# Neighborhood attention on Trainium2: the first load of a band moved behind a turn by DMA, and a V item ahead of a P V

## The chip, the cores and the metric

The kernel runs on one core of a Trainium2 chip. A core has five engines with their own instruction queues: TensorE (PE: matmuls and, overlapping them, weight loads), VectorE (DVE), ScalarE (ACT), GpSimd (POOL) and SyncE (SP). Here SP computes nothing: it issues DMAs, in the order of its queue. Engines wait for each other by semaphores. Matmuls write to PSUM, and VectorE and ScalarE empty it to SBUF. The metric is the device time of one execution in microseconds (us); lower is better.

## The reference: what is computed

An image of 224 x 224 pixels with 192 channels (bf16) gets dilated neighborhood attention: each pixel attends to 7 x 7 = 49 pixels around it, two apart in each direction; at the border the window is pushed inside.

```python
qkv = x @ wqkv
r0 = jnp.clip(ir - half, 0, H - 1 - (ks - 1) * dil)      # half = 6, ks = 7, dil = 2
...
kn = ... # the 49 keys of each pixel, by rows r0 + 2a and columns c0 + 2b
vn = ... # and their values
logits = jnp.einsum('bnc,bnkc->bnk', qf, kn) * scale
p = _softmax(logits, axis=-1)
o = jnp.einsum('bnk,bnkc->bnc', p, vn) @ wo
```

There is one head. The inputs are x (1 x 224 x 224 x 192), wqkv (192 x 576) and wo (192 x 192), all bf16.

## The kernel before, in words

**Tiles.** Since the dilation is two, the image falls into classes of even and odd rows and columns. The work goes over 14 *steps* (seven row tiles times two row classes), each of seven *pairs* m = 0 to 6, 98 pairs k in all. A pair has two strips (`ab` = 0, 1), and each strip has two column classes. The products Wq Wk^T and Wv Wo are formed once at the start, so that a step needs `G` (queries times Wq Wk^T), the image itself as keys (`XA`, `XB`), and `VV` (values times the output weights).

**One pair.** `stage1` (line 499) makes the scores s of a strip on TensorE, with mask rows in the same matmuls, and takes the row maxima nmx on VectorE (line 501). `stage1b` (line 508) makes the exponentials p on ScalarE. `stage2` turns p round, so that it can be a weight of the next matmul. In most pairs that is done by 16 transposes on TensorE (line 538) and a copy from PSUM (line 539); in the pairs that the table `TURN` lists, a DMA transpose issued by SP does it (line 522). In steps 2 to 10 these are pairs 4 and 5 (`turned`), in steps 11 and 12 pairs 2 to 6, in step 13 pairs 0 and 1. `stage3` (line 548) is P V: 16 matmuls for a pair into one of two PSUM buffers for each strip. `stage4` divides by the row sums on VectorE (lines 554 and 571) into one of six output buffers `o_sb`, which SP stores (line 577); the border strip's stores go from GpSimd (line 600).

**Lag.** From k = 14 on the P V of pair k - 3 is done in the turn of the loop for pair k (`values_of`). So P V of pair 5 of a step falls into pair 1 of the next step, and that of pair 4 into pair 0.

**Background work.** While a step's pairs run, the values (`v_item`, lines 335, 338, and the copy out of PSUM at 326 or 328) and the G items (lines 415 and 450) of the next step are made between them. The table `BACK` says which go with which pair: its first entry, if it is not "-", is issued in the middle of the pair (`w64`), the others at its end (`w128`). For pair 1 of a step the entry is "v10e v11 v12e v13e": v10 is the first, in the middle, behind P V. PSUM buffers for these items are three, used in turn. Three moves of values from one row tile's buffer to the other's (`v_over`, line 349) follow the V items 6, 9 and 13; the first two are DMAs from SP in pairs 6 and 0, the third a copy on GpSimd.

**Loads.** A *band* is 16 image rows. `load_items(b)` (lines 145 to 156) gives three DMA transposes from SP (line 154), 448 KB each: for bands from 4 on first the middle 128 channels into `X1[b]`, one of two staging buffers, then the first and the last 128 into `XA`, which is a ring of six bands. At pair 0 of step n the three loads of band n + 3 are made ready, and one is issued at the very end of each of the pairs 0, 1 and 2. From `X1` GpSimd copies the middle channels to `XB` (line 160, at pair 2 of step n for band n + 3) and sorts all three parts into `XS` (line 170) for the V items: for band n + 3 at pairs 2 and 4, and at pair 3 those of band n + 2, in the other class. That copy at pair 3 is the last reader of `X1[n + 2]`.

**Order.** `in_order` keeps every engine's instructions in the order of the program. In SP's queue stand the loads, the turns, the moves of values and the stores of `o_sb`, one behind the other. Each is issued when those ahead of it are issued and its own semaphores are there.

Of the kernel before, what the change touches and what calls it, by code (L numbers as in the profile page):

```python
# [23 lines left out]
NBAND = 14  # L24
# [75 lines left out]
def kernel(  # L100
# [44 lines left out]
    def load_items(b):  # L145

        src = xp[16 * b:16 * b + 16].rearrange("r j c -> (r j) c")
        at = (16 * b) % (2 * RP) * S

        def one(k):  # L150
            if k == 1:
                X1[b] = x1_p.tile([128, BND], BF, name=f"x1_{b}", tag="x1")
            dst = X1[b][:] if k == 1 else XA[k // 2][:, at:at + BND]
            nc.sync.dma_start_transpose(out=dst.unsqueeze(1), in_=src[:, 128 * k:128 * k + 128])  # L154

        return [lambda k=k: one(k) for k in ((0, 2, 1) if b in (0, 2, 3) else (1, 0, 2))]
# [183 lines left out]
    def v_item(rc, ti, cb):  # L340
        def emit(dve):
            pv = ps_g.tile([128, 512], F32, name="pv", tag="pg")
            v_mms(pv, lambda k, h: XS[rc][:, k, cb, 64 * h:64 * h + 64])
            evac(_win(VV[rc][ti % 2], 0, 128, AT[cb] * VP, [[193, 2], [1, C]]), pv[:, 0:2 * C].rearrange("p (t c) -> p t c", c=C), dve)
        return emit

    def v_over(rc, ti, c0, c1, eng=nc.sync.dma_start):

        eng(out=VV[rc][1 - ti % 2][0:64, c0:c1, :], in_=VV[rc][ti % 2][0:64, c0:c1, :])
# [126 lines left out]
    def stage1(J, ab):  # L476
        s = 2 * J.m + ab
        s_ps = SS[ab]


        cols = {0: [(1, 7, S - 7), (8, 8, 0)], 2: [(1, 15, 9)]}.get(s, [(2, 14, 8 * s - 6)])
        lo = cols[0][0]
        for cc in range(2):
            units = []
            for h in range(2):
                u = []
                for pas in range(2):
                    X = (XA, XB)[pas][cc]
                    for (v, k0, n) in key_rows(J, h):
                        for (q, nq, c) in cols:  # L490
                            o = _win(s_ps, 64 * h, 64, cc * 256 + 16 * k0 + q, [[16, n], [1, nq]])
                            u.append((n * nq, o, G[J.rc][cc][:, pas, s, 64 * h:64 * h + 64], _win(X, 0, 128, _x(J.rc, v, c), [[RW, n], [1, nq]]), pas))
                units.append(u)
            done = [0, 0]
            while units[0] or units[1]:
                h = 0 if units[0] and (done[0] <= done[1] or not units[1]) else 1
                (cols_, o, w, r, pas) = units[h].pop(0)
                done[h] += cols_
                nc.tensor.matmul(o, lhsT=w, rhs=r, start=(cc == 0 and done[h] == cols_), stop=(cc == 1 and not units[h]), skip_group_check=True)  # L499
        nmx = stat.tile([128, 2], F32, name="nmx", tag="nmx")  # L500
        nc.vector.tensor_reduce(out=nmx[:], in_=_win(s_ps, 0, 128, lo, [[256, 2], [16, 16], [1, 16 - lo]]), axis=AX.XY, op=ALU.max, negate=True)  # L501
        J.p = PP[J.k % 3]
        J.s[ab] = (s_ps, nmx)
# [9 lines left out]
    def turned(J):  # L513
        return J.m in TURN[J.n]
# [37 lines left out]
    def stage4a(J, ab):  # L552
        J.rs[ab] = stat.tile([128, 2], F32, name="rs", tag="rs")
        nc.vector.reciprocal(out=J.rs[ab][:], in_=J.o_ps[ab][:, C:C + 2])
        return J.rs[ab]
# [55 lines left out]
    def g_all(n):  # L611
        ti, rc = steps[n]
        its = [g_items(rc, ti, s0, ns) for (s0, ns) in GROUPS]
        return [it for (w0, w1, h) in its for it in (w0, w1)], [h for (w0, w1, h) in its]
# [85 lines left out]
    ld, gw, vs = [], [], []  # L700

    def back(it, by_dve):
        it(by_dve)
        for (i, c0, c1) in ((7, 0, 8), (10, 8, 11), (13, 11, 14)) if nb == 0 or nb >= 11 else ((6, 0, 6), (9, 6, 10), (13, 10, 14)):
            if it in vs and it is vs[i]:
                v_over(rcb, tib, c0, c1, pool if nb >= 11 or nb > 0 and i in (13,) else nc.sync.dma_start)

    def values_of(k):

        if k <= 12 or k > 96:  # L710
            return [k - 2] if k >= 2 else []
        return [] if k == 13 else [k - 3, k - 2] if k == 96 else [k - 3]

    for k in range(NP + 2):
        J = pairs[k] if k < NP else None
        n = J.n if J else NSTEP
        w64, w128 = [], []
        if J:
            m = J.m
            nb, mb = divmod(k - LAG, 7)  # L720
            bg = k >= LAG and nb + 1 < NSTEP
            if bg and mb == 0:
                tib, rcb = steps[nb + 1]
                gw, gh = g_all(nb + 1)
                vs = [v_item(rcb, tib, cb) for cb in (0, 1, 2, 3, 4, 5, 6, 13, 7, 8, 9, 10, 11, 12)]
            if n == 0:
                w64 = gh0[m + 1:m + 2] if m < 3 else gh[mb // 2:mb // 2 + 1] if mb % 2 == 0 else []
                w64 = [(it, False) for it in w64]
            elif bg:
                w = [(({"g": gw, "h": gh, "v": vs}[t[0]][int(t[1:].rstrip("de"))], t[-1] == "d" or t[-1] == "e" and turned(pairs[k - 1])) if t != "-" else None) for t in (SECOND if nb == 0 else BACK if nb < 11 else LATE)[mb].split()]  # L730
                w64, w128 = [it for it in w[:1] if it], w[1:]
            stage1(J, 0)
            stage1(J, 1)
            stage1b(J, 0)
            if m == 0 and n + 3 < NBAND:
                ld = load_items(n + 3)
        if k == NP:
            stage2(pairs[k - 1])
        late = [pairs[i] for i in values_of(k)]
        for A in late[:1]:  # L740
            stage3(A, 0)
            stage3(A, 1)
            if k >= NP:
                stage4a(A, 0)
                stage4a(A, 1)
            stage4(A, 0)
            if k == NP - 1:
                stage4a(A, 1)
        for (it, by_dve) in w64:
            back(it, by_dve)  # L750
        if J:
            stage1b(J, 1)
        if J and turned(J):
            stage2(J)
        if 1 <= k < NP and not turned(pairs[k - 1]):
            stage2(pairs[k - 1])

        if late and n > 0:
            stage4(late[0], 1)
        for A in late[1:]:  # L760
            stage3(A, 0)
            stage3(A, 1)
            stage4(A, 0)
            stage4(A, 1)
        if not J:
            continue

        for w in PLAN[m].split() if n == 0 else ():
            (kind, by), at = w.split(":")[0], [int(c) for c in w.split(":")[1:]]
            if kind in "VWGH":  # L770
                {"V": v0, "W": vs, "G": gw0, "H": gw}[kind][at[0]](by == "d")
            elif kind == "N" and late:
                stage4(late[0], 1)
            elif kind == "X":
                xb_items(2, act if by == "a" else dve)[at[0]]()
            elif kind == "R":
                v_over(0, 0, at[0], at[1], nc.scalar.dma_start if by == "a" else nc.sync.dma_start)
            elif kind == "T":
                v_over(rcb, tib, at[0], at[1], nc.scalar.dma_start if by == "a" else nc.sync.dma_start)
        for (it, by_dve) in w128:  # L780
            back(it, by_dve)
        if ld:
            ld.pop(0)()
        if n == 0 and m == 1:
            first_vd()
            g_row_on(1, 2, 12)
            g_col_on()
        for q in range(2):
            if (n, m) == ((1, 3), (1, 5))[q]:
                marks_on(q)  # L790
        add = [it for c in FIRST[k] for it in first_pool(c)] if k < len(FIRST) else []
        if n > 1:
            if m == 3 and n + 2 < NBAND:
                add = sort_items(n + 2, J.rc, pool)
            if m in (2, 4) and n + 3 < NBAND:
                srt = sort_items(n + 3, J.rc, pool)
                add = srt[:2] if m == 4 else xb_items(n + 3, pool) + srt[2:]
        pool_q[:0] = add
        if n == 12 and m == 1:
            last = ((0, 9, 0, 1), (9, 7, 9, 0))  # L800
            g_col(1, 6, 0, 1, pool)
            g_row(1, 6, 0, 1, pool, last)
            g_row(1, 6, 1, 13, pool, last[1:])
        pool_do(max(4 if n < NSTEP - 1 else 8, len(add)))
# [34 lines left out]
```

## Time and profile before

| | |
|---|---|
| median of 3 runs | 338.47 us (338.19 to 339.24) |
| the profiled execution's own time | 340.54 us |
| its span, first to last instruction | 338.8 us |
| granted TensorE clock, mean | 0.994 |
| busy: TensorE, VectorE, ScalarE, GpSimd | 318.8, 310.4, 306.3, 286.4 us |
| SP's DMA queue, share of 16 DMA engines | 82.9% |

Times in a view are microseconds from the start of the span. A row of a timeline has the start, the duration, engine and line, the operation, the tile written <- the tiles read, the shapes, and how many instructions were merged into the row; in brackets the idle time before it and who ended it. "SPq" is SP's queue: its duration runs from when the queue comes to the instruction to when the DMA is issued, not to its landing. A row of waits has total, times and longest. A row of the chain of waits has start, duration and what the end of the program waited for at that time; a "DMA" row there runs from the issue to the landing.

### The profile page before, as it was taken

What the parts mean: (1) busy time and instruction counts of PE and PEld (TensorE: products, weight loads), DVE (VectorE), ACT (ScalarE), POOL (GpSimd) and SP (SyncE); (2) the same over time, 40 slices, a digit from 0 to 9 for tenths busy, and PEclk for the clock granted to TensorE, in tenths of its full rate; (3) what the DMA queues carried; (4) which work ended last, traced back from release to release, by engine and by line L of the source; (5) the groups of instructions that cost most, each with busy time, mean ns of one, the idle gap of its engine ahead of it and who ended that gap; (6) DMA issues with size and microseconds to landing.
All of it is one profiled execution on the core that took longest, in us unless ns stands there. A gap on an engine that the chain in (4) does not pass through costs nothing.

```text
span 338.8 us, 18840 instructions
## 1 busy us (share of the span) xinstructions
PE 318.8 (94%) x7820; PEld 291.3 (86%) x7820; DVE 310.4 (92%) x730; ACT 306.3 (90%) x807; POOL 286.4 (85%) x428
## 2 busy tenths in 40 slices
PE   4499999999999999999999999999999999999982
PEld 2378898999999999998999999988899889999871
DVE  8759999989999999998999999999999989999992
ACT  7679899999999999898999999999999989999982
POOL 8399999899989969889698897994996978997664
PEclk9999999999999999999999999999999999999997
DMA  8999745999979998899997998979879978959634
GB/s 173 207 194 185 140 99 127 196 226 183 168 186 188 176 192 155 158 206 146 166 183 165 179 180 186 160 160 190 160 162 177 159 177 131 143 111 161 130 100 100
DMA packets 143368, 55.78 MB, mean 165 GB/s; under 512 B 117113, under 2 KB 141138, under 8 KB 143283
## 3 DMA queue, kind: packets, MB, share of 16 engines
q1 hardware_dynamic: 138207, 51.98, 82.9%
q0 software_dynamic: 4416, 1.81, 2.9%
q8 instruction: 61, 1.00, 1.3%
q10 hardware_dynamic: 660, 0.80, 1.0%
q14 instruction: 24, 0.20, 0.2%
HBM read 0.29 MB, written 19.27 MB: 58 GB/s over the span
## 4 chain that ended last, share of the span: by engine, by line
PE 73%; ACT 8%; DMA 4%; DVE 4%; SPq 3%; issue 3%; POOL 2%; POOLq 0%; DVEq 0%; ACTq 0%
PE s L499 16%; PE o_ps L548 15%; PE pg L415 12%; PE pv L335 9%; PE pv L338 8%; PE pt_ps L538 7%; PE pgh L415 6%; ACT p L508 5%; SPq L154 3%; DMA pt_sb<-p 3%; DVE nmx L501 2%; POOL out_dram L600 2%; ACT v L328 2%; DMA xa<-in_x_dram 2%; ACT gx L328 1%
## 5 line engine op out<-in xcount | busy, mean ns | idle before, releaser
L508 ACT ACTIVATE p<-s,nmx 128x256 bf16<-128x256 f32 x392 | 163.1, 485 | 17.8 <-DVE nmx L501 15.3
L501 DVE TENSOR_REDUCE nmx<-s 128x2 f32<-128x448 f32 (+1 forms) x196 | 114.3, 624 | 9.8 <-PE s L499 5.6
L571 DVE TENSOR_TENSOR o_sb<-o_ps,rs 128x384 bf16<-128x384 f32 x169 | 94.2, 557 | 6.1 <-DMA out_dram<-o_sb 0.2
L499 PEld LDWEIGHTS <-g 128*64 128x64 bf16 x2592 | 86.5, 110 | 6.5 <-issue 1.4
L328 ACT CAST v<-pv 128x384 bf16<-128x384 f32 x180 | 85.0, 512 | 3.0 <-PE pv L338 2.8
L499 PE MATMUL s<-xa,g 128*64 128x112 bf16 (+8 forms) x1296 | 82.6, 217 | 0.8 <-ACT p L508 0.8
L499 PE MATMUL s<-xb,g 128*64 128x112 bf16 (+8 forms) x1296 | 82.4, 217 | 0.2 <-ACT g L328 0.2
L548 PE MATMUL o_ps<-v,pt_sb 128*64 128x193 bf16 x1456 | 81.1, 246 | 1.3 <-DMA pt_sb<-p 0.7
L335 PE MATMUL pv<-wb,xs 128*64 128x384 bf16 x406 | 73.6, 331 | 3.8 <-ACT xs L360 3.3
L338 PE MATMUL pv<-wp,xs 128*64 128x192 bf16 x812 | 74.3, 248 | 0.6 <-issue 0.6
L450 POOL COPY g<-gx 64x512 bf16<-64x512 bf16 (+1 forms) x110 | 61.6, 560 | 14.6 <-ACT gx L328 10.5
L600 POOL DMA_DIRECT2D out_dram<-o_s x120 | 68.1, 574 | 3.6 <-issue 2.6
L548 PEld LDWEIGHTS <-pt_sb 128*64 128x64 bf16 x1456 | 66.2, 109 | 2.2 <-DMA pt_sb<-p 1.1
L415 PEld LDWEIGHTS <-aw 128*64 128x64 bf16 x1320 | 58.3, 111 | 10.4 <-issue 4.0
L338 PEld LDWEIGHTS <-xs 128*64 128x64 bf16 x812 | 59.0, 111 | 6.6
L328 ACT CAST g<-pg 128x512 bf16<-128x512 f32 (+4 forms) x130 | 53.6, 479 | 2.6 <-PE pg L415 1.8
L415 PE MATMUL pg<-xa,aw 128*64 128x512 bf16 (+9 forms) x440 | 53.2, 273 | 2.6 <-DMA xa<-in_x_dram 1.7
L415 PE MATMUL pg<-xb,aw 128*64 128x512 bf16 (+9 forms) x440 | 54.8, 272 | 0.0
L170 POOL COPY xs<-xa 128x896 bf16<-128x896 bf16 x51 | 46.5, 939 | 6.2 <-DMA xa<-in_x_dram 5.3
L538 PE MATMUL pt_ps<-ident,p 128*64 128x128 bf16 x1072 | 45.2, 219 | 0.0
L539 DVE COPY pt_sb<-pt_ps 128x1024 bf16<-128x1024 bf16 x63 | 42.9, 681 | 0.5 <-PE pt_ps L538 0.5
L160 POOL COPY xb<-x 64x1792 bf16<-64x1792 bf16 x22 | 36.9, 1676 | 7.4 <-DMA x<-in_x_dram 6.7
(78 smaller groups left out, 358.2 us busy)
## 6 DMA issues: line engine op xcount, KB each, us to landing
out_dram<-o_sb SPq DMA_DIRECT2D x156, 96.0 KB
v<-v SPq DMA_DIRECT2D x10, 289.5 KB
v<-v SPq DMA_DIRECT2D x10, 193.0 KB
out_dram<-o_sb SPq DMA_DIRECT2D x13, 78.0 KB
xb<-xb SPq DMA_DIRECT2D x2, 448.0 KB
out_dram<-xs SPq DMA_DIRECT2D x11, 72.0 KB
v<-v SPq DMA_DIRECT2D x2, 337.8 KB
out_dram<-o_s POOLq DMA_DIRECT2D x26, 18.0 KB, 3.6
```

Of the source, the lines that this page charges most:

```text
L328: nc.scalar.copy(out=out_, in_=in_)
L335: nc.tensor.matmul(pv[64 * h:64 * h + 64, 0:2 * C], lhsT=at(1, h), rhs=WB[:].rearrange("p t c -> p (t c)"), start=True, stop=False, skip_g ...
L338: nc.tensor.matmul(pv[64 * h:64 * h + 64, cc * C:(cc + 1) * C], lhsT=at(2 * cc, h), rhs=WP[(cc, 0)], start=False, stop=True, skip_group_ch ...
L415: nc.tensor.matmul(o, lhsT=l, rhs=r, start=(pas == 0), stop=(pas == 1))
L450: nc.gpsimd.tensor_copy(out=G[rc][cc][p:p + 64, 1, s0:s0 + ns, :], in_=gx[p:p + 64, 0:ns * 128].rearrange("p (s q) -> p s q", q=128))
L499: nc.tensor.matmul(o, lhsT=w, rhs=r, start=(cc == 0 and done[h] == cols_), stop=(cc == 1 and not units[h]), skip_group_check=True)
L501: nc.vector.tensor_reduce(out=nmx[:], in_=_win(s_ps, 0, 128, lo, [[256, 2], [16, 16], [1, 16 - lo]]), axis=AX.XY, op=ALU.max, negate=True)
L508: nc.scalar.activation(out=J.p[:, ab, cc].rearrange("p q (r k) -> p q r k", k=8), in_=_win(s_ps, 0, 128, cc * 256, [[8, 2], [16, 16], [1, ...
L538: nc.tensor.transpose(pt_ps[64 * h:64 * h + 64, 4 * ab + 2 * cc + q, :], J.p[:, ab, cc, q, 64 * h:64 * h + 64], ident[:])
L548: nc.tensor.matmul(o_ps[64 * h:64 * h + 64, cc * 193:cc * 193 + 193], lhsT=J.pt[:, 4 * ab + 2 * cc + q, 64 * h:64 * h + 64], rhs=V[h][:, A ...
L571: nc.vector.tensor_tensor(out=o_sb[:], in0=_win(o_ps, 0, 128, 0, [[194, 2], [1, C]]), in1=rs[:].unsqueeze(2).to_broadcast([128, 2, C]), op ...
L600: pool_q.append(lambda dst=dst, p=p, m=n * nj, cc=cc: nc.gpsimd.dma_start(out=dst, in_=o_sb[p:p + m, cc, :]))
```

## The change

It has two parts.

First, for bands 6 to 13 the three loads are issued one place earlier each. At pair 5 of step n, from step 2 on, the loads of band n + 4 are made ready, and the first is issued at the end of that pair, behind the turn of pair 5 and the pair's stores. Nothing is issued at pair 6. The second and third follow at the ends of pairs 0 and 1 of step n + 1. Bands 3, 4 and 5 keep pairs 0, 1 and 2 of steps 0, 1 and 2.

Second, where the P V to be done belongs to a pair that was turned by DMA in steps 2 to 10, the item in the middle of the pair is issued before P V. For the P V of pair 4 the entry of the table is "-", so nothing moves; for that of pair 5 it is v10.

```diff
             stage1b(J, 0)
-            if m == 0 and n + 3 < NBAND:
+            if m == 5 and n > 1 and n + 4 < NBAND:
+                ld = load_items(n + 4)
+            elif m == 0 and n < 3:
                 ld = load_items(n + 3)
         if k == NP:
             stage2(pairs[k - 1])
         late = [pairs[i] for i in values_of(k)]
+        if late and turned(late[0]) and 2 <= late[0].n < 11:
+            for (it, by_dve) in w64:
+                back(it, by_dve)
+            w64 = []
         for A in late[:1]:
             stage3(A, 0)
             stage3(A, 1)
...
         for (it, by_dve) in w128:
             back(it, by_dve)
-        if ld:
+        if ld and (m < 6 or n < 2):
             ld.pop(0)()
```

## The prediction

> **What bounds the kernel now.** I read the page first, then the lengths of the steps, then TensorE's waits, the chain of waits, and the queues of SP, VectorE and GpSimd around the places that these named. From the page:
>
> ```profile
> span 338.8 us, 18840 instructions
> ...
> PE 318.8 (94%) x7820; PEld 291.3 (86%) x7820; DVE 310.4 (92%) x730; ACT 306.3 (90%) x807; POOL 286.4 (85%) x428
> ...
> DMA  8999745999979998899997998979879978959634
> ...
> q1 hardware_dynamic: 138207, 51.98, 82.9%
> ```
>
> TensorE is busy 94% of the span, and the DMA engines are nearly as full: 82.9% go to the one queue that SP issues. A step begins with the row maximum (line 501) of its pair 0. In order of time, steps 3, 4, 8, 9 and 10 begin here (timeline of VectorE):
>
> ```profile
> 91.30 0.66 DVE L501 TENSOR_REDUCE nmx<-s 128x2 f32<-128x480 f32 x1
> ...
> 113.02 0.66 DVE L501 TENSOR_REDUCE nmx<-s 128x2 f32<-128x480 f32 x1
> ...
> 201.58 0.66 DVE L501 TENSOR_REDUCE nmx<-s 128x2 f32<-128x480 f32 x1
> ...
> 223.30 0.66 DVE L501 TENSOR_REDUCE nmx<-s 128x2 f32<-128x480 f32 x1
> ...
> 245.33 0.66 DVE L501 TENSOR_REDUCE nmx<-s 128x2 f32<-128x480 f32 x1
> ```
>
> Step 3 takes 113.02 - 91.30 = 21.72 us and step 8 takes 223.30 - 201.58 = 21.72 us, equal to the hundredth although the DMA traffic beside them differs. So a step goes at TensorE's pace, and only what stops TensorE counts. Step 9 takes 245.33 - 223.30 = 22.03 us, 0.31 us more. The waits of TensorE say why (in us: total, times, longest):
>
> ```profile
> PE o_ps L548 <- DMA pt_sb<-p: 0.7, 1, 0.7
> ...
> PEld L548 <- DMA pt_sb<-p: 1.1, 2, 0.9
> ...
> PE pv L338 <- issue: 0.6, 1, 0.6
> ```
>
> The weight loads of P V (line 548) waited twice for a turn by DMA, 0.9 and 0.2 us, 1.1 us together. The chain of waits names the two places, and shows an undisturbed case first (start, us):
>
> ```profile
> 116.36 0.72 PE o_ps L548 x16
> ...
> 221.82 4.92 DMA pt_sb<-p
> ...
> 226.78 0.86 PE o_ps L548 x16
> ...
> 267.11 4.47 DMA pt_sb<-p
> ...
> 271.63 0.86 PE o_ps L548 x16
> ```
>
> Both are the turns of pair 5, of steps 8 and 10. From its issue such a turn needs 4.5 to 4.9 us until it has landed. Now SP's own queue, which issues loads (154), turns (522), moves of values (349) and stores (577) in program order: step 3, then the end of step 5, step 8, and steps 9 to 10.
>
> ```profile
> 110.06 1.26 SPq L522 DMA_TRANSPOSE pt_sb<-p  x1
> ...
> 117.45 2.15 SPq L154 DMA_TRANSPOSE x<-in_x_dram  x1
> ...
> 158.49 3.31 SPq L577 DMA_DIRECT2D out_dram<-o_sb  x3
> ...
> 213.27 3.52 SPq L154 DMA_TRANSPOSE xa<-in_x_dram  x1
> ...
> 221.82 2.30 SPq L522 DMA_TRANSPOSE pt_sb<-p  x1
> ...
> 246.05 1.19 SPq L577 DMA_DIRECT2D out_dram<-o_sb  x2
> ...
> 252.17 2.09 SPq L154 DMA_TRANSPOSE x<-in_x_dram  x1
> ...
> 256.52 1.65 SPq L154 DMA_TRANSPOSE xa<-in_x_dram  x1
> 258.27 1.19 SPq L577 DMA_DIRECT2D out_dram<-o_sb  x2
> 259.51 2.68 SPq L154 DMA_TRANSPOSE xa<-in_x_dram  x1
> 262.28 1.19 SPq L577 DMA_DIRECT2D out_dram<-o_sb  x2
> ```
>
> In step 3 the turn of pair 5 is issued at 110.06 and used at 116.36, 6.3 us later: 1.4 us to spare over 4.9. In step 8 it is issued 221.82 - 201.58 = 20.24 us after the step began, in step 3 18.76 us after (110.06 - 91.30): SP was 1.5 us later than in step 3, and the 1.4 us were gone. It was late because loads before it took long (213.27: 3.52 us instead of the 1.65 of 256.52).
>
> **The change, part by part.** *The V item ahead of P V.* At pair 1 of steps 3 to 11, the item v10 (six matmuls) is issued before the 16 of P V of the preceding step's pair 5, not behind them. What it costs on TensorE:
>
> ```profile
> 271.63 0.86 PE L548 MATMUL o_ps<-v,pt_sb 128*64 128x193 bf16 x16 [0.71 <-DMA pt_sb<-p]
> 272.33 0.33 PE L335 MATMUL pv<-wb,xs 128*64 128x384 bf16 x2
> 272.49 0.33 PE L338 MATMUL pv<-wp,xs 128*64 128x192 bf16 x4
> 272.65 0.61 PE L538 MATMUL pt_ps<-ident,p 128*64 128x128 bf16 x16
> ```
>
> It takes 272.65 - 272.33 = 0.32 us. Where the turn is on time, the order of two pieces changes and TensorE's sum does not: zero. VectorE gets P V 0.32 us later, but it has two row maxima of the same pair to do first, 0.66 us each as above, longer than the delay: zero, and 0.32 us a pair if that cover were gone. ScalarE's own order stays (exponentials, v10, exponentials); v10 only reaches it earlier. The PSUM buffer of v10 is one of three and was last used three items before; were it not yet free, the gain of the next sentence would go, no more. Where the turn is late, v10 fills the wait: at 226.78 all of the 0.2 us, at 271.63 0.32 of the 0.9. Together 0.2 + 0.32 = 0.5 us, lower bound 0 and upper bound 2 x 0.32 = 0.64.
>
> *The loads.* For bands 6 to 13 the three loads stand behind pair 5 of the step before, pair 0 and pair 1, where they stood behind pairs 0, 1 and 2. Nothing is added; on SP the first load passes about four stores and two moves of values, the others two stores each. What was issued before a turn of pair 4 or 5 is the same set as before: all three loads of that step's band. SP works first in, first out, so a turn gets earlier only by what SP used to stand idle while the first load waited for its place in the program. In step 5 there is such a time: three stores at 158.49 took 3.31 us where two take 1.19 (246.05), so about 1.5 us were spent waiting for stores to become ready, and the load would now lie in it. From step 8 on nothing like it is left, and a later pause, where SP catches up with the program, eats some of it. I take a third of the 1.5, 0.5 us earlier, for the turns of steps 8 and 10. That frees the second wait (0.9 - 0.32 = 0.58) of some 0.5. Ends: 0 (no gain is left by then) and 0.58.
>
> A load can be issued only when its staging buffer is free. The first load of band n+4 takes the buffer whose last reader is GpSimd's copy xs<-x queued at pair 3 of step n. (The other two loads write a ring of six bands, over a band whose last reader is some two steps back: no wait.) In steps 9 and 10:
>
> ```profile
> 244.30 0.93 POOL L170 COPY xs<-x 128x896 bf16<-128x896 bf16 x1
> ...
> 258.29 3.39 POOL L160 COPY xb<-x 64x1792 bf16<-64x1792 bf16 x2 [2.65 <-DMA x<-in_x_dram]
> ```
>
> The copy xs<-x ends at 245.23; SP would come to the load behind the two stores of 246.05, at 247.3, 2.1 us later: no wait. If GpSimd lagged more, SP would stand, and all stores behind it with it. On the other side the copies of line 160, which waited 2.65 us for their load in step 10, find it landed. GpSimd is off TensorE's path (no wait of TensorE names it), so I count nothing.
>
> *What is late next.* Stores behind the first load leave later by that load's time: 2.1 us (252.17), minus the 0.5 that SP is ahead, 1.6 us. Each holds one of six output buffers. How much room there is, VectorE shows:
>
> ```profile
> 252.86 0.56 DVE L571 TENSOR_TENSOR o_sb<-o_ps,rs 128x384 bf16<-128x384 f32 x1
> ...
> 257.31 0.56 DVE L571 TENSOR_TENSOR o_sb<-o_ps,rs 128x384 bf16<-128x384 f32 x1
> ...
> 263.29 0.56 DVE L571 TENSOR_TENSOR o_sb<-o_ps,rs 128x384 bf16<-128x384 f32 x1
> ...
> 266.51 0.56 DVE L571 TENSOR_TENSOR o_sb<-o_ps,rs 128x384 bf16<-128x384 f32 x1 [0.23 <-DMA out_dram<-o_sb]
> ```
>
> The output of 257.31 goes, counted in order, with the first of the two stores of 262.28, which is through at 262.88; its buffer is taken again by the sixth output behind it, at 266.51, which had to wait 0.23 us. So a store needs up to 3.6 us from its issue to landing. The output of 252.86 goes, counted in order, with the first of the two stores of 258.27, through at 258.87, and its buffer is wanted again at 263.29: 4.4 us of room there. After the change that store stands behind the third load too. With 1.6 us more, 2.8 us are left, and up to 3.6 are needed: a wait of up to 0.8 us on VectorE, in the busiest places of steps 8 and 9. Its bounds: no wait (a store that finds the DMA engines free), and 0.8 at each of two places, 1.6. How much of it TensorE feels no row shows; with two P V buffers between them it is not more than the whole. I take a quarter of the upper end, 0.4 us of loss in all, since the nearest row, 266.51, is a wait of only 0.23.
>
> By the Trainium skill, page "DMA: Bandwidth & Descriptors", section "Latency and other measured facts", a DMA transpose moves about 261 GB/s; a load of 128 x 1792 bf16 elements, 458,752 bytes, would by an estimate from that take 1.76 us, less than the 2.09 us of issue here, and the room lost would be 0.3 us smaller; no row here has the transport alone. The same page, section "Queues, rings and completion order", says that on each DMA engine descriptors are consumed in the order of the ring; the turn that stands ahead of the load is then not delayed by it, while the stores behind it are, which is the mechanism of the slower rival below; the trace agrees as far as it goes, since the turn of 221.82, with two stores close behind it, landed in 4.92 us.
>
> Sum: -0.5 (V item) - 0.5 (turns) + 0.4 (stores) = -0.6 us. The profiled execution took 340.54 us, its span 338.8; the median without profile is 338.47, 2.07 below. On the profiled execution the sum gives 339.9; carried to the median 337.9. That step assumes that the timed executions have the same two waits, which no row shows.
>
> **The rivals.** *A, more than the waits of the turns goes, faster.* Both waits vanish (1.1 us) and so does the 0.6 us for which TensorE stood at a V item with nothing in the profile to name ("issue"), while turns and loads filled the DMA engines. Then 338.47 - 1.1 - 0.6 = 336.8. For it: the DMA engines get two pairs of rest, 2 and 3, ahead of the turns. Against it: the work ahead of each turn is the same, and only SP's idle time can be won.
>
> *B, the stores take the place of the turns, slower.* It decides where a store of pairs 6 to 2 is delayed by a whole load and the engines have no idle time: 0.8 us of room missing at two places in each of steps 7, 8 and 9, all of it passed on to TensorE through the two P V buffers in PSUM, is 6 x 0.8 = 4.8, of which half hidden leaves 2.4; less the 0.5 of the V item: 338.47 + 1.9 = 340.4. It wins over the gain from about 1.0 us of stalls on. For it: the room of 4.4 us and the wait of 0.23. Against it: a wait for a buffer slows VectorE's next outputs and gives SP time to catch up.
>
> *C, nothing.* The timed executions have no late turn (the median is 2.07 us below the profiled one, more than the waits add up to), and the stores fit: 338.5, inside the forecast's band.
>
> **How the numbers follow.** About 0.3%, 1.0 us, is what a measurement of this kernel can tell from no change. The forecast together with C, between 337.5 and 339.4, has 0.5; A 0.27; B 0.23. The forecast is 337.9, with a range of its own of 337.0 to 339.0. The whole range reaches towards A's 336.8 and B's 340.4 and leaves out a tenth at each side: 336.7 to 340.0.
>
> **What would show it.** Right: no wait of line 548 for pt_sb at pair 1; in SP's queue a load behind each turn of pair 5 of steps 2 to 9, without long waits for GpSimd; line 160 no longer waits for its load; steps 3, 8 and 9 at 21.72 us. Wrong: waits of line 571 for out_dram<-o_sb of more than 1 us in total, or steps 6 to 10 above 21.72 with VectorE idle ahead of an output (B); the 0.6 us of "issue" gone as well (A); or the turn of pair 5 landing later because the load behind it shares its DMA time.

## The result, and the profile after

The changed kernel is slower. Its median is 340.20 us (338.11 to 342.94) against 339.09 us (337.40 to 340.92) for the kernel before on the same chip: a ratio of 1.0035, 95% interval 1.0018 to 1.0052. On a second chip it was 340.35 against 338.55 us, 1.0044 (1.0026 to 1.0062). So it loses 1.1 to 1.8 us. The ratios are taken from the single executions and differ a little from the quotient of the medians. Executions more than 1.5% above the fastest of the same kernel are left out of a ratio: three of twelve of "the loads alone" below (344.1 to 344.7 us, the profiled one among them; with them its mean would be 0.4% above that of the kernel before) and one each of two other kernels (347.7 and 348.8 us).

The single executions matter here. Over more of them the kernel before spreads from 337.4 to 340.9 us; the profiled one, 340.54 us, is among its slower ones, and the profiled execution of the changed kernel, 340.08 us, is an ordinary one of that kernel. From the start of step 2 to the end of the span the two profiles even take the same time (338.8 - 69.58 = 269.2 us before, 338.3 - 68.96 = 269.3 us after). They differ in *where* they lose time, and that is what they are read for.

The page of the changed kernel, the lines that answer to those of before:

```profile
span 338.3 us, 18823 instructions
...
PE 319.9 (95%) x7820; PEld 294.4 (87%) x7820; DVE 310.6 (92%) x730; ACT 306.9 (91%) x807; POOL 287.2 (85%) x428
...
DMA  9999745989898996996999979899989758959734
...
q1 hardware_dynamic: 138207, 51.98, 80.8%
```

The work is the same: equal bytes and packets in SP's queue. Now SP's queue in steps 8 and 10 of the changed kernel (start, us, line):

```profile
221.16 1.26 SPq L522 DMA_TRANSPOSE pt_sb<-p  x1
...
223.16 2.19 SPq L154 DMA_TRANSPOSE x<-in_x_dram  x1
...
264.72 1.67 SPq L522 DMA_TRANSPOSE pt_sb<-p  x1
```

and the row maxima with which steps 3, 4, 5, 8, 9 and 10 begin (timeline of VectorE; a row with x2 merges two instructions):

```profile
91.36 1.19 DVE L501 TENSOR_REDUCE nmx<-s 128x2 f32<-128x480 f32 x2
...
114.11 1.19 DVE L501 TENSOR_REDUCE nmx<-s 128x2 f32<-128x480 f32 x2
...
136.25 1.19 DVE L501 TENSOR_REDUCE nmx<-s 128x2 f32<-128x480 f32 x2
...
202.62 0.66 DVE L501 TENSOR_REDUCE nmx<-s 128x2 f32<-128x480 f32 x1
...
224.34 1.19 DVE L501 TENSOR_REDUCE nmx<-s 128x2 f32<-128x480 f32 x2
...
246.06 0.66 DVE L501 TENSOR_REDUCE nmx<-s 128x2 f32<-128x480 f32 x1
```

The turn of pair 5 is now issued 221.16 - 202.62 = 18.54 us after step 8 begins, and 264.72 - 246.06 = 18.66 us after step 10 begins. Before it was 20.24 us in step 8, and 267.11 - 245.33 = 21.78 us in step 10 up to the DMA of the chain. The load of the next band stands behind the turn (223.16). Steps 8 and 9 take 21.72 us each. That part of the change does what it says. But step 3 takes 114.11 - 91.36 = 22.75 us, 1.03 us more than the 21.72 before. The waits of TensorE and VectorE (total, times, longest) name one that has grown, from 0.2 us in the kernel before, and a new one:

```profile
DVE o_sb L571 <- DMA out_dram<-o_sb: 1.2, 1, 1.2
PE o_ps L548 <- DMA v<-v: 1.1, 2, 0.8
```

No wait of P V for `pt_sb` is left. In its place P V waits for `v<-v`, a *move of values*. In order of time (TensorE, then VectorE, then SP, in step 3, and the second wait of TensorE, in step 5):

```profile
101.83 0.86 PE L548 MATMUL o_ps<-v,pt_sb 128*64 128x193 bf16 x16 [0.78 <-DMA v<-v]
...
146.29 0.86 PE L548 MATMUL o_ps<-v,pt_sb 128*64 128x193 bf16 x16 [0.31 <-DMA v<-v]
```

```profile
100.07 0.56 DVE L571 TENSOR_TENSOR o_sb<-o_ps,rs 128x384 bf16<-128x384 f32 x1 [1.22 <-DMA out_dram<-o_sb]
```

```profile
92.82 1.73 SPq L154 DMA_TRANSPOSE x<-in_x_dram  x1
94.64 0.55 SPq L577 DMA_DIRECT2D out_dram<-o_sb  x1
95.28 0.55 SPq L349 DMA_DIRECT2D v<-v  x1
95.92 2.47 SPq L577 DMA_DIRECT2D out_dram<-o_sb  x3
98.49 0.56 SPq L349 DMA_DIRECT2D v<-v  x1
99.10 1.71 SPq L154 DMA_TRANSPOSE xa<-in_x_dram  x1
...
142.28 0.50 SPq L349 DMA_DIRECT2D v<-v  x1
```

The same place in the kernel before, SP's queue and TensorE:

```profile
95.45 0.56 SPq L349 DMA_DIRECT2D v<-v  x1
96.10 2.59 SPq L154 DMA_TRANSPOSE x<-in_x_dram  x1
...
100.73 0.25 PE L548 MATMUL o_ps<-v,pt_sb 128*64 128x193 bf16 x1
```

Before, the second move of values of step 3 (95.45) went out *ahead* of the step's first load (96.10). Now the first load (92.82) stands ahead of both moves, and the second one leaves at 98.49, 7.13 us after the step began instead of 95.45 - 91.30 = 4.15. P V of pair 0 is due 100.73 - 91.30 = 9.43 us after the step began, in pair 3. It reads three column blocks of the values: with `AT` as it is, places 7, 0 and 1 of `VV`, since block 13 sits in place 7. Places 0 to 5 come with the first move, but place 7 comes with the second (places 6 to 9). The two waits above ended 101.83 - 98.49 = 3.3 us and 146.29 - 142.28 = 4.0 us after the issue of the move. So, by an estimate from these two waits, it must be issued within 9.43 - 4.0 = 5.4 to 9.43 - 3.3 = 6.1 us of the step's start. From the starts of line 349 and of the steps in the three traces (the third kernel is the experiment "swap", below), issue of the second move after its step's start, us:

| step | 3 | 4 | 5 | 6 | 7 | 8 | 9 | 10 |
|---|---|---|---|---|---|---|---|---|
| before | 4.15 | 3.78 | 3.80 | 3.78 | 4.58 | 4.23 | 5.61 | 5.28 |
| changed | 7.13 | 5.12 | 6.03 | 5.69 | 5.50 | 5.04 | 5.16 | 6.17 |
| swap | 9.29 | 5.90 | 5.80 | 5.36 | 6.52 | 6.68 | 6.62 | 6.22 |

Before, 0.8 us (step 7, by the tighter limit) to 2.3 us were left in steps 3 to 8. The change spends them, and in steps 3 and 5 more than them. (Step 10 of the changed kernel, at 6.17, shows no wait, so the limit is not sharp.) The transfers are the same; one with a near due time was put behind one with a far one.

By the Trainium skill, page "DMA: Bandwidth & Descriptors", section "Queues, rings and completion order", descriptors are consumed in the order of the ring on each DMA engine, though a later one may finish its write before an earlier one. The rows show the order of issue alone, and agree as far as that goes: with the load in front the move is issued 3.0 us later, and P V, which waits for it, starts 1.0 us after it was due.

One number is used below for all kernels: the *loss at a pair*. For each pair, take the time from its first row maximum to that of the next pair, less the shortest such time of the same pair in all traces here but those of the two kernels that issue the move from ScalarE, and add up steps 3 to 10. This P V stands in pair 3: before, the loss there is 0.4 us, in the changed kernel 1.2 us, and in its profile on the second chip 3.3 us. Pair 2 ends when VectorE comes to the row maximum of pair 3, and there its wait at line 571 stands (1.22 us above, 0.80 us on the second chip): the loss at pair 2 is 0.0 us before, 1.0 and 0.6 us in the two profiles of the changed kernel. Against that stand the losses at pairs 0 and 1 of steps 3 to 11, where turns are waited for: 1.6 us before, 0.4 and 0.4 us in the two profiles of the changed kernel.

### The profile page after: what moved, and what is told of

It is laid out like the page before. It is cut to its first block, busy times and chain, and to the rows that moved or that the text cites. A ratio compares the mean times of both kernels' runs of the same rounds, so it can differ in the third digit from the quotient of the medians.

```text
span 338.3 us, 18823 instructions
## 1 busy us (share of the span) xinstructions
PE 319.9 (95%) x7820; PEld 294.4 (87%) x7820; DVE 310.6 (92%) x730; ACT 306.9 (91%) x807; POOL 287.2 (85%) x428
## 4 chain that ended last, share of the span: by engine, by line
PE 74%; ACT 9%; DVE 4%; DMA 4%; SPq 3%; POOL 2%; issue 2%; POOLq 0%; DVEq 0%; ACTq 0%
PE s L499 16%; PE o_ps L548 16%; PE pg L415 13%; PE pv L335 9%; PE pv L338 8%; PE pt_ps L538 6%; PE pgh L415 6%; ACT p L508 5%; SPq L154 3%; ACT v L328 2%; DVE nmx L501 2%; DMA v<-v 2%; POOL out_dram L600 2%; DMA xa<-in_x_dram 2%; ACT g L328 1%
## 5 line engine op out<-in xcount | busy, mean ns | idle before, releaser
L335 PE MATMUL pv<-wb,xs 128*64 128x384 bf16 x406 | 74.7, 333 | 3.7 <-ACT xs L360 3.2
L338 PE MATMUL pv<-wp,xs 128*64 128x192 bf16 x812 | 75.1, 250 | 0.0
L415 PEld LDWEIGHTS <-aw 128*64 128x64 bf16 x1320 | 60.0, 111 | 7.9 <-issue 1.8
L338 PEld LDWEIGHTS <-xs 128*64 128x64 bf16 x812 | 61.0, 112 | 5.8
L415 PE MATMUL pg<-xb,aw 128*64 128x512 bf16 (+9 forms) x440 | 55.6, 272 | 0.0
L415 PE MATMUL pg<-xa,aw 128*64 128x512 bf16 (+9 forms) x440 | 54.0, 273 | 1.3 <-ACT gx L328 0.9
L335 PEld LDWEIGHTS <-xs 128*64 128x64 bf16 x406 | 33.8, 111 | 8.2 <-ACT xs L360 3.5
```

What stands on the lines that cost most here:

```text
L335: nc.tensor.matmul(pv[64 * h:64 * h + 64, 0:2 * C], lhsT=at(1, h), rhs=WB[:].rearrange("p t c -> p (t c)"), start=True, stop=False, skip_g ...
L338: nc.tensor.matmul(pv[64 * h:64 * h + 64, cc * C:(cc + 1) * C], lhsT=at(2 * cc, h), rhs=WP[(cc, 0)], start=False, stop=True, skip_group_ch ...
L415: nc.tensor.matmul(o, lhsT=l, rhs=r, start=(pas == 0), stop=(pas == 1))
```

## The experiments

Two theories for the loss. *Moves*: the second move of values is late for P V at pair 3. *Stores* (the mechanism of rival B): stores behind the load hold the output buffers, VectorE waits at line 571. In step 3 of the profile above both waits stand side by side at 100 us, and each may hide the other, so only an edit can tell them apart; in step 5 the move is late with no such wait of VectorE. All ratios are against the kernel before on the same chip; its median there stands with them, since its medians differ by up to 0.7% from chip to chip.

**Each part alone.** The loads alone (part 1 of the diff), and the V item alone (part 2):

```diff
-        if late and turned(late[0]) and 2 <= late[0].n < 11:      # loads alone
-            for (it, by_dve) in w64:
-                back(it, by_dve)
-            w64 = []
```

> The first part of the change alone: the loads moved, the V item left behind P V. The measured change is +1.2 us. Moves theory (the second move of values, issued in pair 0, now stands behind the first load in SP's queue and lands too late for the P V in pair 3): the loss stays, +1 to +1.5 us against before, and line 548 waits for v<-v at pair 3 in some steps. Stores theory (output buffers run out because stores stand behind the first load): the same time, but line 571 waits for out_dram<-o_sb in several steps. V item theory (P V 0.32 us later holds VectorE up): this kernel is as fast as before, within 0.3 us.

> The second part alone: v10 ahead of the P V of pair 5, the loads where they were. Moves and stores theories: no loss, 0 to -0.6 us against before, the late turns at pair 1 partly filled. V item theory: +1 us or more.

The loads alone: 341.39 against 340.89 us, 1.0010 (0.9975 to 1.0045), which separates nothing. The V item alone: 340.03 us, 0.9996 (0.9962 to 1.0029): no effect that can be told, so nothing shows that the V item costs or wins. Its profile has a wait for `v<-v` too, one of 1.5 us at pair 3 of step 2, where all kernels have their loads in the same places: the second move can be late without the change.

**One more output buffer, to take the stores' wait away.** The seventh `o_sb` is paid for with one of the border strip's buffers.

```diff
-            o_sb = work.tile([128, 2, C], BF, name="o_sb", tag="o_sb", bufs=6)
+            o_sb = work.tile([128, 2, C], BF, name="o_sb", tag="o_sb", bufs=7)
...
-            o_sb = work.tile([128, 2, C], BF, name="o_s0", tag="o_s0")
+            o_sb = work.tile([128, 2, C], BF, name="o_s0", tag="o_s0", bufs=1)
```

> The changed kernel with seven output buffers o_sb instead of six; the border strip's buffer o_s0, used once a step, is one instead of two, which makes the room. Stores theory: the waits of line 571 for out_dram<-o_sb go, and the time falls by about 1 us, to that of before. Moves theory: no change against the changed kernel (+0.8 to +1.5 us against before), and the waits of line 548 for v<-v stay.

The changed kernel with it: 342.06 against 340.89 us, 1.0048 (1.0018 to 1.0079). Its waits, where no row of line 571 for `out_dram` is left:

```profile
PE o_ps L548 <- DMA v<-v: 1.2, 3, 0.6
```

Without a wait for stores the moves are still waited for, three times, and the loss at pair 3 is 2.6 us. So the wait for stores isn't needed for that loss. The time by itself decides less, as the same edit on the kernel before shows:

> The kernel before with seven output buffers o_sb and one o_s0. One look: no wait of line 571 for out_dram<-o_sb, no wait of GpSimd or VectorE for the single o_s0, waits of line 548 as in the kernel before. If VectorE waits for o_s0 here, the single buffer itself costs, and the seven-buffer version of the changed kernel says nothing on stores.

One execution took 341.31 us where the kernel before has a median of 339.53 us, so the edit may have a price of its own. Its profile says where:

```profile
DVE o_s L571 <- issue: 1.7, 1, 1.7
PE o_ps L548 <- DMA v<-v: 0.8, 2, 0.6
```

VectorE stands 1.7 us ahead of the border strip's output, which now has a single buffer (in step 1; 1.1 us in the changed kernel with it, and no such row in the kernel before), though the profile doesn't name what it waits for. And P V waits twice for a move (steps 2 and 6) with the loads in their old places; the loss at pair 3 is 1.2 us where the kernel before has 0.4. By the condition set above, the time of the seven-buffer kernel then says nothing on the stores, and part of its 2.6 us may be the edit's.

**The cut of the moves, so that place 7 comes with the first move.** The second move is then issued a pair later and first needed a pair later.

```diff
-        for (i, c0, c1) in ((7, 0, 8), (10, 8, 11), (13, 11, 14)) if nb == 0 or nb >= 11 else ((6, 0, 6), (9, 6, 10), (13, 10, 14)):
+        for (i, c0, c1) in ((7, 0, 8), (10, 8, 11), (13, 11, 14)):
```

> The changed kernel with the moves of values cut elsewhere: positions 0 to 7 in the first move (pair 6), 8 to 10 in the second (pair 1), 11 to 13 on GpSimd, as steps 0 and 11 on have it, instead of 0 to 5, 6 to 9 and 10 to 13. Pair 0 reads positions 7, 0 and 1, so its P V (in pair 3) needs the first move only. Moves theory: no wait of line 548 for v<-v at pair 3, and the time is 1 to 1.5 us below the changed kernel, at or a little under before (-0.5 to +0.2 us). Stores theory: no gain, +0.8 to +1.5 us against before.

> The kernel before with the other cut of the moves (0 to 7, 8 to 10, 11 to 13), loads and V item as before. Moves theory: pair 3 never waits for v<-v; where the loads stand behind both moves that gains little, 0 to -1 us (the rare wait of step 2). If the cut itself costs (a first move of 386 KB instead of 289), it shows here as +1 us or more, and then the cut explains why the changed kernel with it was not faster.

> The V item part of the change and the other cut of the moves, the loads where they were before. Moves theory: no wait at pair 3, and the late turns at pair 1 are partly filled: -0.5 to -1.5 us against before, the fastest of all. Stores theory and V item theory: no gain, within 0.3% of before or slower.

> The loads part of the change with the other cut of the moves (0 to 7, 8 to 10, 11 to 13). The cut alone cost +0.7% (before_mv). Moves theory: with this cut P V of pair 3 does not read what the second move brings, so the shift of the loads costs nothing more: +0.3 to +0.7% against before, not more than before_mv. Stores theory: the shift adds its own cost, +1.0% or more.

The changed kernel with it: 341.78 against 340.89 us, 1.0047 (1.0010 to 1.0085). The kernel before with it: 341.69 against 339.53, 1.0071 (1.0046 to 1.0096). The V item alone with it: 341.13, 1.0052 (1.0023 to 1.0081). The loads alone with it: 341.56 against 339.80, 1.0038 (1.0007 to 1.0070). The cut has a price of its own, 0.7% in the kernel before. With it, neither part of the change nor both together are slower than the kernel before with it. In the profile of the changed kernel the P V at pair 3 still waits once, in step 4, now for the larger *first* move, and beside it VectorE waits for a store:

```profile
124.73 0.86 PE L548 MATMUL o_ps<-v,pt_sb 128*64 128x193 bf16 x16 [1.14 <-DMA v<-v]
```

```profile
123.04 0.56 DVE L571 TENSOR_TENSOR o_sb<-o_ps,rs 128x384 bf16<-128x384 f32 x1 [1.64 <-DMA out_dram<-o_sb]
```

In that of the loads alone with the cut it stood 2.1 us in step 5, and the profile names nothing that it waited for. The ratios fit the moves, but the edit's own price and these waits make it a poor test.

**The swap: the kernel before, with nothing but the first load and the second move exchanged in SP's queue.** No load is taken earlier by a pair.

```diff
+        if ld and m == 0 and n > 2:
+            ld.pop(0)()
         for (it, by_dve) in w128:
             back(it, by_dve)
-        if ld:
+        if ld and (m > 0 or n < 3):
             ld.pop(0)()
```

> The kernel before, with one thing changed: in pair 0 of steps 3 to 10 the first load is issued just ahead of the second move of values instead of just behind it. Stores, turns and the other loads keep their places. Moves theory: that move lands 1.5 to 2.6 us later (the first load's time in SP's queue); its room before was between 0.5 us (steps 9, 10) and 1.8 us (step 4), so P V at pair 3 waits for v<-v in most steps 3 to 10, in sum 3 to 10 us, and the time rises by as much (+1 to +3%). Stores theory: the time stays within 0.3%, since no store has moved.

347.95 (four executions) against 339.53 us: 1.0236 (1.0187 to 1.0286), some 8 us. Its waits, SP's queue in step 3, and TensorE there:

```profile
PE o_ps L548 <- DMA v<-v: 3.3, 6, 2.1
```

```profile
97.47 3.44 SPq L154 DMA_TRANSPOSE x<-in_x_dram  x1
101.00 0.54 SPq L349 DMA_DIRECT2D v<-v  x1
```

```profile
104.51 0.86 PE L548 MATMUL o_ps<-v,pt_sb 128*64 128x193 bf16 x16 [2.15 <-DMA v<-v]
```

The loss at pair 3 is 8.3 us, in step 3 alone 4.0, and it stands in all of the steps 5 to 10 as well. The wait for stores is 0.2 us in all. So this one order alone, move ahead of load, is worth 2.4%; the changed kernel has the wrong order too, but its load is issued two pairs earlier, so that the move behind it is less late (the table above).

**The second move from ScalarE's queue**, where no load stands in front of it:

```diff
-                v_over(rcb, tib, c0, c1, pool if nb >= 11 or nb > 0 and i in (13,) else nc.sync.dma_start)
+                v_over(rcb, tib, c0, c1, pool if nb >= 11 or nb > 0 and i in (13,) else nc.scalar.dma_start if i == 9 else nc.sync.dma_start)
```

> The changed kernel with the second move of values (positions 6 to 9, pair 0) issued from ScalarE's queue instead of SP's, so that it no longer stands behind the first load; nothing else is changed. Moves theory: no wait of line 548 for v<-v at pair 3 in steps 3 to 10, and about 1 us less than the changed kernel, that is 0 to -1 us against before, unless the issue of 0.55 us on ScalarE costs (seen in before_act). Stores theory: no gain, +0.8 to +1.5 us against before.

> The kernel before with the second move issued from ScalarE's queue. It is the price of that alone: the issue takes ScalarE 0.55 us in each of ten steps, with some 0.25 us of idle time a pair. Moves theory: within 0.3% of before, and after_act not slower than this one. If it is 1 us or more slower, the issue on ScalarE costs, and only the difference between the two kernels speaks on the loads.

The changed kernel with it: 342.67 against 339.80 us, 1.0094 (1.0063 to 1.0125). The kernel before with it: 343.03 us, 1.0097 (1.0065 to 1.0130). The issue on ScalarE costs 1%, which makes it no remedy. But with the move out of SP's queue no difference between the two can be told any more, and no wait for `v<-v` is left in either. The profile of the changed kernel with it shows what a wait for a store does by itself, at the place of step 3 where the two waits stood side by side:

```profile
100.06 0.56 DVE L571 TENSOR_TENSOR o_sb<-o_ps,rs 128x384 bf16<-128x384 f32 x1 [0.89 <-DMA out_dram<-o_sb]
```

```profile
101.94 0.52 PE L548 MATMUL o_ps<-v,pt_sb 128*64 128x193 bf16 x8 [0.21 <-DVE o_sb L571]
```

The second half of P V at pair 3 (8 of its 16 matmuls) waits for VectorE, and pair 2 is some 0.6 us longer than in the other steps. So a wait for a store can cost by itself, and of the loss of step 3 in the profile of the changed kernel a good part is likely the stores'.

**Another order of the blocks, so that P V at pair 3 needs the first move alone.** Block 13 is put in place 0 and computed first. Moves, bytes and queue stay as they are.

```diff
-AT = (0, 1, 2, 3, 4, 5, 6, 8, 9, 10, 11, 12, 13, 7)
+AT = (1, 2, 3, 4, 5, 6, 7, 8, 9, 10, 11, 12, 13, 0)
...
-                vs = [v_item(rcb, tib, cb) for cb in (0, 1, 2, 3, 4, 5, 6, 13, 7, 8, 9, 10, 11, 12)]
+                vs = [v_item(rcb, tib, cb) for cb in (13, 0, 1, 2, 3, 4, 5, 6, 7, 8, 9, 10, 11, 12)]
```

> The changed kernel with the values kept in another order of places: column block 13 first (place 0, computed first), then blocks 0 to 12, where block 13 was at place 7 between blocks 6 and 7. The moves stay as they are (places 0 to 5, 6 to 9, 10 to 13, same bytes, same queue). Pair 0 reads blocks 13, 0 and 1, so the P V of pair 3 now needs the first move only. Moves theory: no wait of line 548 for v<-v at pair 3, and the loss of the change goes: -0.5 to +0.2 us against before. Stores theory: the loss of about 1 us stays.

> The kernel before with that order of places alone. Moves theory: 0 to -0.6 us against before (the rare waits of pair 3 go, the late turns of pair 5 stay), and the changed kernel with this order is as fast or up to 1 us faster than this. If it is slower than before by more than 0.3%, the order itself costs.

> The loads part and the order of places. Moves theory: with pair 3 free of the second move, the shift of the loads costs nothing: within 0.3% of before_13, no wait for v<-v at pair 3. Stores theory: slower than before_13 by about 1 us.

> The V item part and the order of places, the loads where they were before. Moves theory: like before_13 or up to 0.6 us less (late turns partly filled): 0 to -1 us against before.

> The swap (first load ahead of the second move in pair 0 of steps 3 to 10) with block 13 in place 0. The swap alone cost +2.4%. Moves theory: P V of pair 3 no longer needs that move, so the cost of the swap goes nearly whole: within 0.5% of before. If half or more of the 2.4% stays, the swap hurts by something else that stands behind the load.

> The changed kernel itself, beside the same runs of the kernel before as swap_13 and on one chip with it. Moves theory: again slower than before, +0.2 to +0.5%, with waits for v<-v at pair 3, which the changed kernel with block 13 in place 0 did not have (1.0006 there). If it comes out at 1.000, the loss is too small to be told from the spread of the executions.

| kernel | as it is | with the order of blocks | loss at pair 3, as it is and with it (us) | at pair 2 (us) |
|---|---|---|---|---|
| before | 1 | 1.0004 (0.9982 to 1.0026) | 0.4, 0.4 | 0.0, 0.0 |
| V item alone | 0.9996 (0.9962 to 1.0029) | 0.9984 (0.9964 to 1.0005) | 0.4, 0.4 | 0.0, 0.0 |
| loads alone | 1.0010 (0.9975 to 1.0045) | 1.0000 (0.9974 to 1.0025) | -, 0.2 | -, 0.4 |
| changed | 1.0035 (1.0018 to 1.0052), 1.0044 (1.0026 to 1.0062) | 1.0006 (0.9981 to 1.0030) | 1.2 and 3.3, 0.2 | 1.0 and 0.6, 0.2 |
| swap | 1.0236 (1.0187 to 1.0286) | 1.0031 (1.0009 to 1.0054) | 8.3, 0.3 | 0.0, 0.0 |

The medians with the order were 340.05 us for the changed kernel, 340.41 for the kernel before, 340.28 for the loads alone and 339.37 for the V item alone (before: 340.03 on that chip), and 340.26 for the swap (before: 338.55 on its chip). The order by itself costs nothing, takes some seven eighths of the swap's loss away, and all of the changed kernel's that can be measured. The profile of the swap with this order shows it most sharply. Step 3: its first row maximum on VectorE, SP's queue, and P V at pair 3 on TensorE:

```profile
90.55 1.19 DVE L501 TENSOR_REDUCE nmx<-s 128x2 f32<-128x480 f32 x2
```

```profile
94.44 3.39 SPq L154 DMA_TRANSPOSE x<-in_x_dram  x1
97.93 0.54 SPq L349 DMA_DIRECT2D v<-v  x1
```

```profile
99.98 0.25 PE L548 MATMUL o_ps<-v,pt_sb 128*64 128x193 bf16 x1
100.07 0.76 PE L548 MATMUL o_ps<-v,pt_sb 128*64 128x193 bf16 x14
```

The load still stands in front, for 3.39 us, and the second move is issued 97.93 - 90.55 = 7.38 us after the step's start, as late as in the changed kernel. P V starts at 99.98, 9.43 us after the step's start, on time and only 2.05 us after the move's issue, less than the 3.3 to 4.0 us after which the two waits above ended. The lateness is still there; only nobody needs the move yet. The changed kernel as it is, on the second chip, shows the place once more:

```profile
101.77 0.86 PE L548 MATMUL o_ps<-v,pt_sb 128*64 128x193 bf16 x16 [1.12 <-DMA v<-v]
```

So the moves account for nearly all of the swap's cost and, by the ratios with the order of blocks, for most of the changed kernel's loss. Four things stay open. How much of that loss is the stores' isn't settled: in its profiles they have the loss at pair 2, 1.0 and 0.6 us, and with the order of blocks, where 0.2 us of it is left, the time is that of the kernel before within the interval. The 0.3% that the swap keeps with the order of blocks has no wait in its profile to name it; the profiled execution, 337.43 us, is its fastest. How the changed kernel's loss divides between its parts isn't measured: the loads alone came out at 1.0010, with an interval that holds both 1 and the whole loss. And the step from 1.0035 and 1.0044 to 1.0006 has an uncertainty of about 0.003 in itself; it is the swap, with a step of 0.02, that makes it firm. The V item with the order of blocks has the lowest ratio, 0.9984, but its interval reaches over 1, so no version here is shown to beat the kernel before.

## Why the prediction was wrong

It said 337.9 us and most likely no measurable change; it came out 0.35 to 0.44% slower, with 340.20 us just above the range.

**The bound.** Right. Steps 8 and 9 go at 21.72 us in the changed kernel too, and the losses at pair 3 stand where TensorE waits.

**The loads, on SP: the step that failed.** It said that "on SP the first load passes about four stores and two moves of values", and then priced the stores alone. The moves were named and given no cost and no cover. Had the same question been put to them as to the stores (who needs this, when, and how long does it take to land), the rows of before would have given most of the answer: move issued at 95.45, P V at 100.73, 5.3 us apart, against a load that takes 2.1 to 2.6 us of the queue. How long a move takes to land no row of before says; the two waits after the change put it at 3.3 to 4.0 us, which leaves 1.3 to 2.0 us to spare, and the turns' 4.5 to 4.9 us would have left less. The sum lacked a term for this, 0.8 and 0.3 us of waiting in steps 3 and 5 of the profile, partly offset elsewhere by SP's being ahead.

**The turns earlier.** Right in direction and much too small in size. The turns of pair 5 are issued 1.7 us (step 8) and some 3 us (step 10) earlier after the step's start, not 0.5, because SP starts each step's loads sooner and has made up its arrears by the turns: counted in order, the stores of pairs 3 and 4 in steps 8 to 10 are issued 0.6 to 2.1 us after VectorE has made the output in the changed kernel, where it was 2.4 to 5.2 us before. The waits at pair 1 of steps 9 and 11 are gone. But what there was to win was read from one execution. In other profiles of kernels with the loads in their old place the waits for turns lie elsewhere: of the V item alone at 94.63 us (0.82 us), of the kernel before with the order of blocks at 113.57 (0.84) and 271.47 us (0.24). So "the timed executions have the same two waits, which no row shows" was the second weak step. The loss at pairs 0 and 1 fell from 1.6 to 0.4 us in the profiles, but not for every kernel with the loads in their new place: the changed kernel with the order of blocks waited 1.24 us at 92.31 us for a turn of pair 4. So how much of such a wait a typical execution has is not settled; it is less than what the moves and the stores take.

**The V item.** Right that it costs nothing, 0.9996. Its 0.5 us did not show, within 0.4%; with the turns on time it has nothing to fill.

**What is late next: the stores.** The mechanism exists, the place was wrong. The wait of line 571 is 1.2 us, once, in step 3, where steps 7 to 9 were named; on the second chip 0.8 us. It passed the bound set for rival B. With a seventh buffer the wait goes and P V's waits for moves stay, and with the order of blocks the changed kernel still waits 0.6 us for stores at line 571 and loses nothing to the kernel before that can be measured. Yet such a wait is not free: the 0.4 us of loss allowed for it stand against 1.0 and 0.6 us at pair 2 in the two profiles. B had the sign and almost the time (340.4), by a mechanism that is a part of it at most, so the nearness of the number is luck.

**The staging buffer.** Right: SP didn't stand for GpSimd's copy, and the copies of line 160 from step 3 on wait for no load (2.65 and 2.08 us at their longest before). As said, that was worth nothing.

**The median and the profile.** The 2.07 us between the profiled execution and the median of three were carried over as if they told profiled and timed executions apart. Over more executions the median is 339.09, and the profiled one, 340.54, lies within their spread.

## What to carry to other kernels

When a DMA is issued earlier in an in-order queue, list everything that it now stands in front of, with the due time of each at its reader and the time from issue to landing; the one with the least to spare pays, and it need not be the kind of transfer that the change was about. A late transfer can often be made harmless without touching the queue, by laying the data out so that the block needed first comes with the transfer that goes first: here two lines, at no cost. And where executions of one kernel spread by 1%, the waits of a single profile are samples: a gain that rests on two of them is worth less than it shows.

## What was not expected of the hardware

- The exchange of two neighbouring DMAs in one queue cost 2.4% (the swap). The load in front took 3.44 us of the queue in step 3, where the move took 0.54.
- Ten DMAs issued from ScalarE instead of SP cost 1.0% (343.03 against 339.80 us), with 0.47 us of ScalarE's queue each, 4.7 us in all. By the Trainium skill, page "DMA: Bandwidth & Descriptors", section "Issuing engines are not separate DMA queues", another issuing engine saves only the time to initiate a DMA, which is usually small beside the DMA itself; here, on an engine that is 90% busy, it was large enough to lose by: a step with no other loss (step 8 of the kernel before with the moves there) takes 226.40 - 204.46 = 21.94 us, not 21.72. A row of the kernel before with the moves there (ScalarE's queue):

```profile
116.73 0.47 ACTq L349 DMA_DIRECT2D v<-v  x1
```

- A first move of 8 places instead of 6 (with 3 instead of 4 in the second) and the second issued a pair later cost 0.7% in the kernel before, with no more matmuls on TensorE. Which wait this is was not settled.
